# A decode kernel bound by its loads: the result row kept in two PSUM tensors, copied by two engines and stored by SyncE in 16 runs, with the projections summed in place

## Chip, cores, metric

One core of one Trainium2 chip. The metric is device time in microseconds (us) of one execution. "The span" is the time from the first to the last instruction in the profile; the measured time is longer than the span (402.11 against 400.3 us in the profiled run of the kernel before). One TensorE (PE) works with VectorE (DVE), ScalarE (ACT), GpSimd (POOL) and SyncE (SP).

## The reference, cut to what matters

One token of a decoder layer: grouped-query attention over a cache of 65536 keys (32 query heads, 4 key/value heads), and beside it an MLP; both are added to the input row.

```python
def _A_ref(x, k_cache, v_cache, wq, wo):      # attention
    q = (x @ wq)...                           # 32 heads of 128
    p = _softmax(einsum(q, k) * Dh ** -0.5)
    o = einsum(p, v)
    return o.reshape(B, Sq, Hq * Dh) @ wo     # "the projections": one per head
# [... _B_ref: ... gelu(layernorm(x1) @ w3) @ w4 ...]
return x + _A_ref(xn, ...) + _B_ref(xn, ...)  # one row of 1024 bf16
```

## The kernel before

Weights and cache go through three big SBUF slots in a fixed order: wq, w3, w1 and w2, then K and V blocks 0 to 7 (wo before the last V), and at the end w4 in 8 pieces. Everything that is added to the output row is added by matmuls into one PSUM tensor `psB`: the first 512 results on partition 0, the second 512 on partition 32, where PE's two column positions work side by side. Only the projections of the first three groups go elsewhere and are added later.

```python
def row_acc(j, lhsT, rhs, start=False):
    nc.tensor.matmul(psB[32 * j:32 * j + lhsT.shape[1], :], lhsT=lhsT, rhs=rhs, start=start, stop=False,
                     tile_position=(0, 32 * j), skip_group_check=True)
# [...]
def project(g):
    wt = st.tiles["wo"][:].rearrange("p (g j n) -> p g j n", g=HKV, j=8)
    for j in range(8):
        for h2 in range(2):
            if g == HKV - 1:
                row_acc(h2, oT[g][:, j:j + 1], wt[:, g, j, 512 * h2:512 * (h2 + 1)])
                continue
            nc.tensor.matmul(tail["rows"][0:1, h2, :], lhsT=oT[g][:, j:j + 1], rhs=wt[...], ...,
                             tile_position=(0, 0))

def add_projection():
    rows = ppool.tile([1, 2, 512], F32, name="o_rows", tag="p")
    nc.vector.tensor_copy(out=rows[:], in_=tail["rows"][0:1, 0:2, :])
    for j in range(2):
        row_acc(j, ident_f[0:1, 0:1], rows[0:1, j, :])
# [...]
compute_k(NU - 1)
tail["rows"] = ps_S.tile([P, SUBS, 512], F32, name="o_acc", tag="sc")
for g in range(HKV - 1):
    project(g)
add_projection()
compute_v(NU - 1)
early = sum(W4_PIECES[:2])                    # W4_PIECES = (6, 5, 6, 4, 3, 2, 1, 1)
compute_w4(0, early)
project(HKV - 1)
compute_w4(early, FC)

out_t = ogpool.tile([64, 512], BF16, name="out_t", tag="og")
nc.scalar.copy(out=out_t[:], in_=psB[0:64, :])
nc.scalar.dma_start(out=out[0, 0, :].rearrange("(j n) -> j n", j=2),
                    in_=out_t[:].rearrange("(a b) n -> a b n", b=32)[:, 0, :])
```

Of the kernel before, what the change touches and what calls it, by code (L numbers as in the profile page):

```python
# [8 lines left out]
BF16 = mybir.dt.bfloat16  # L9
F32 = mybir.dt.float32  # L10
# [5 lines left out]
P = 128  # L16
ROW = 32768
SUBS = 4
# [45 lines left out]
def kernel(  # L64
# [14 lines left out]
    nc = tc.nc  # L79
# [4 lines left out]
    HKV = A_k_cache.shape[1]  # L84
# [17 lines left out]
    ppool = ctx.enter_context(tc.tile_pool(name="psb", bufs=1))  # L102
    ogpool = ctx.enter_context(tc.tile_pool(name="og", bufs=2))
    ps_S = ctx.enter_context(tc.tile_pool(name="psS", bufs=1, space=bass.MemoryType.PSUM))
# [63 lines left out]
    ident_f = const.tile([P, P], F32, name="ident_f")  # L168
# [9 lines left out]
    for b in range(2):  # L178
        nc.gpsimd.tensor_copy(
            out=spread[:, 2 * b:2 * b + 2, :].rearrange("p r (a i) -> p r a i", a=4),  # L180
            in_=ident_f[:, 64 * b:64 * b + 64].rearrange("p (i r) -> p r i", r=2).unsqueeze(2).to_broadcast([P, 2, 4, 32]))
# [5 lines left out]

    psB = ps_B.tile([P, 512], F32, name="psB")

    def row_acc(j, lhsT, rhs, start=False):  # L190
        nc.tensor.matmul(psB[32 * j:32 * j + lhsT.shape[1], :], lhsT=lhsT, rhs=rhs, start=start, stop=False,  # L191
                         tile_position=(0, 32 * j), skip_group_check=True)

    x_t = ppool.tile([P, DC, 32], BF16, name="x_t", tag="p")
    for a in range(4):
        nc.vector.transpose(out=x_t[32 * a:32 * a + 32].rearrange("p c j -> p (c j)"),  # L196
                            in_=x_row[:, 256 * a:256 * (a + 1)].rearrange("p (i c) -> p c i", c=DC))
# [3 lines left out]
    def layernorm(src, tag):  # L201
# [39 lines left out]
                          in_=sel8[:].unsqueeze(2).to_broadcast([P, 8, 16]))  # L241
# [36 lines left out]
    def place_queries(g):  # L278
        for a in range(4):
            at = slice(32 * a, 32 * a + 32)  # L280
            nc.gpsimd.tensor_copy(  # L281
                out=qdiag[at, LEAD:].rearrange("p (x c) -> p x c", x=4)[:, :, 32 * a:32 * a + 8],
                in_=qx[at, :, 8 * g:8 * g + 8])
# [31 lines left out]
    def compute_k(u):  # L315
        g, b = divmod(u, NB)
        if b == 0:
            place_queries(g)
            group["nball"] = const.tile([P, NB], F32, name=f"nball{g % 2}")
            group["lall"] = const.tile([P, NB], F32, name=f"lall{g % 2}")  # L320
        t = st.tiles[("K", u)]
        cols = t[:].rearrange("p (s u k b x r) -> p s u k b x r", u=SUBS, s=SETS, k=16, b=2, r=2)
        sc = ps_S.tile([P, SUBS, 512], F32, name="sc", tag="sc")
        W = ROW // SETS
        for s in range(SETS):
            words = t[:, W * s:W * (s + 1)].bitcast(F32)
            nc.vector.transpose(out=words, in_=words)  # L327
            for b2 in range(2):
                for r in range(2):
                    c0 = LEAD + P * (2 * b2 + r) - 8 * s  # L330
                    for e in range(SUBS):
                        nc.tensor.matmul(sc[:, e, :], lhsT=qdiag[:, c0:c0 + P], rhs=cols[:, s, e, :, b2, :, r],  # L332
                                         start=(s == 0 and b2 == 0 and r == 0),
                                         stop=(s == SETS - 1 and b2 == 1 and r == 1))
        st.done(("K", u))
        mx = small.tile([P, 1], F32, name="mx")
        nc.vector.reduce_max(out=mx[:], in_=sc[:].rearrange("p e n -> p (e n)"), axis=AX.X)  # L337
        pm = ps_M.tile([P, 512], F32, name="pm_mx", tag="pm")
        nc.tensor.transpose(pm[0:1, 0:P], mx[:, 0:1], ident_f[:])  # L339
        m8 = small.tile([1, 8], F32, name="m8")  # L340
        nc.vector.tensor_reduce(out=m8[:], in_=pm[0:1, 0:P].rearrange("o (j h) -> o h j", h=8), axis=AX.X, op=ALU.max)  # L341
        rep = small.tile([1, P], F32, name="rep")
        nc.vector.tensor_scalar(out=rep[:].rearrange("o (j h) -> o j h", h=8),  # L343
                                in0=m8[:].unsqueeze(1).to_broadcast([1, P // 8, 8]), scalar1=-SCALE, scalar2=None,
                                op0=ALU.mult)
        nc.tensor.transpose(pm[:, P:P + 1], rep[0:1, :], ident_f[0:1, 0:1])  # L346
        nball = group["nball"]
        nc.vector.tensor_copy(out=nball[:, b:b + 1], in_=pm[:, P:P + 1])  # L348
        p_sb = ppool.tile([P, SUBS, 512], BF16, name="p_sb", tag="p")
        nc.scalar.activation(out=p_sb[:], in_=sc[:], func=ACTF.Exp, bias=nball[:, b:b + 1], scale=SCALE,  # L350
                             accum_out=group["lall"][:, b:b + 1])
        flat = p_sb[:].rearrange("p e n -> p (e n)")
        nc.vector.transpose(out=flat, in_=flat)  # L353
        group["p"] = p_sb

    def group_weights():
        nball = group["nball"]
        negmg = small.tile([P, 1], F32, name="negmg")
        nc.vector.tensor_reduce(out=negmg[:], in_=nball[:], axis=AX.X, op=ALU.min)
        wb = small.tile([P, NB], F32, name="wb")  # L360
        nc.scalar.activation(out=wb[:], in_=nball[:], func=ACTF.Exp, bias=negmg[:, 0:1], scale=-1.0)
        og = group["og"]
        nc.vector.tensor_scalar(out=og[:], in0=og[:], scalar1=wb[:, 0:1], scalar2=None, op0=ALU.mult)
        lw = small.tile([P, NB], F32, name="lw")
        ol = small.tile([P, DH + 1], F32, name="ol")
        nc.vector.tensor_tensor_reduce(out=lw[:], in0=group["lall"][:], in1=wb[:], scale=1.0, scalar=0.0,
                                       op0=ALU.mult, op1=ALU.add, accum_out=ol[:, DH:DH + 1])
        return og, wb, ol
# [3 lines left out]
    def compute_v(u):  # L372
        g, b = divmod(u, NB)
        if b == 1:
            og, wb, ol = group_weights()
        vt = st.tiles[("V", u)][:].rearrange("p (s u t d) -> p s u t d", u=SUBS, s=SETS, t=16)
        oacc = ps_O.tile([P, 512], F32, name="oacc")
        pT = group["p"]
        for e in range(SUBS):
            for t in range(16):  # L380
                q = t % 4
                nc.tensor.matmul(oacc[32 * q:32 * (q + 1), :], lhsT=pT[:, e, 32 * t:32 * (t + 1)],  # L382
                                 rhs=vt[:, :, e, t, :], start=(e == 0 and t < 4),
                                 stop=(e == SUBS - 1 and t >= 12), tile_position=(0, 32 * q))
        st.done(("V", u))
        if b == 0:
            og = ogpool.tile([P, 512], F32, name="og", tag="og")
            nc.scalar.copy(out=og[:], in_=oacc[:])
            group["og"] = og
            return  # L390
        nc.vector.scalar_tensor_tensor(out=og[:], in0=oacc[:], scalar=wb[:, 1:2], in1=og[:],  # L391
                                       op0=ALU.mult, op1=ALU.add)
        group_rows(g, og, ol)

    oT = {}
    tail = {}

    def group_rows(g, og, ol):
        pe = ps_M.tile([P, 512], F32, name="pm_e", tag="pm")
# [14 lines left out]
    def project(g):  # L414
        wt = st.tiles["wo"][:].rearrange("p (g j n) -> p g j n", g=HKV, j=8)
        for j in range(8):
            for h2 in range(2):
                if g == HKV - 1:
                    row_acc(h2, oT[g][:, j:j + 1], wt[:, g, j, 512 * h2:512 * (h2 + 1)])
                    continue  # L420
                nc.tensor.matmul(tail["rows"][0:1, h2, :], lhsT=oT[g][:, j:j + 1],  # L421
                                 rhs=wt[:, g, j, 512 * h2:512 * (h2 + 1)], start=(g == 0 and j == 0),
                                 stop=(g == HKV - 2 and j == 7), tile_position=(0, 0))

    def add_projection():
        rows = ppool.tile([1, 2, 512], F32, name="o_rows", tag="p")
        nc.vector.tensor_copy(out=rows[:], in_=tail["rows"][0:1, 0:2, :])  # L427
        for j in range(2):
            row_acc(j, ident_f[0:1, 0:1], rows[0:1, j, :])

    def compute_w4(lo, hi):
        wt = st.tiles["w4"]
# [7 lines left out]
    for u in range(NU - 1):  # L440
        compute_k(u)
        compute_v(u)
    compute_k(NU - 1)
    tail["rows"] = ps_S.tile([P, SUBS, 512], F32, name="o_acc", tag="sc")
    for g in range(HKV - 1):
        project(g)
    add_projection()
    compute_v(NU - 1)
    early = sum(W4_PIECES[:2])
    compute_w4(0, early)  # L450
    project(HKV - 1)
    compute_w4(early, FC)

    out_t = ogpool.tile([64, 512], BF16, name="out_t", tag="og")
    nc.scalar.copy(out=out_t[:], in_=psB[0:64, :])
    nc.scalar.dma_start(out=out[0, 0, :].rearrange("(j n) -> j n", j=2),
                        in_=out_t[:].rearrange("(a b) n -> a b n", b=32)[:, 0, :])

# [1 line left out]
_INS = ['A_x', 'A_k_cache', 'A_v_cache', 'A_wq', 'A_wo', 'B_x', 'B_w1', 'B_w2', 'B_w3', 'B_w4']  # L460
# [26 lines left out]
```

## Time and profile before

Median 402.27 us (402.11 to 402.31, 3 runs). The profiled run took 402.11 us.

| | before |
|---|---|
| span | 400.3 us |
| PE, DVE busy | 59%, 52% |
| loads | 169.87 MB at 424 GB/s, 98.6% of the 16 DMA engines' span |
| last load of w4 lands | 396.73 us |
| last pair of matmuls to issue of the store | 396.77 to 397.80 us |

From the chain that ended last, its end (start us, us, what):

```profile
338.78 40.54 DMA big<-in_A_v_cache_dram
...
379.33 17.39 DMA big<-in_B_w_dram
396.73 0.04 issue
396.77 0.40 PE psB L191 x2
...
397.19 0.58 ACT out_t L455
```

The last V block lands at 379.32, the last piece of w4 at 396.73. From the timeline of the last 34 us, in order (start us, us, engine, line, operation, count, and in brackets idle time before it and what ended it):

```profile
367.50 12.19 PE L421 MATMUL o_acc<-big,oT 128*1 128x512 bf16 x45 [2.40 <-ACT p_sb L350]
...
383.86 1.21 DVE L427 COPY o_rows<-o_acc 1x1024 f32<-1x1024 f32 x1 [13.62 <-PE oacc L382]
385.00 0.73 DVE L391 SCALAR_TENSOR_TENSOR og<-oacc,wb,og 128x512 f32<-128x512 f32 x1
...
386.21 2.30 PE L191 MATMUL psB<-big,hT 128*1 128x512 bf16 x10
...
395.47 1.03 PE L191 MATMUL psB<-big,hT 128*1 128x512 bf16 x6 [0.27 <-DMA big<-in_B_w_dram]
...
396.77 0.38 PE L191 MATMUL psB<-big,hT 128*1 128x512 bf16 x2 [0.27 <-DMA big<-in_B_w_dram]
397.19 0.58 ACT L455 CAST out_t<-psB 64x512 bf16<-64x512 f32 x1 [29.56 <-PE psB L191]
397.80 0.59 ACTq L456 DMA_DIRECT2D out_dram<-out_t  x1
```

The projections (L421) run in PE's wait for V. Then the copy of the projection row (L427) holds up VectorE and, through its adding matmuls, PE (1.33 us of waiting for the copy): the w4 matmuls start only at 386.21. But at 395.47 and 396.77 PE has nothing to do and waits 0.27 us for the DMA each time: it has caught up.

### The profile page before, as it was taken

The page shows a single profiled execution, that of the slowest core. Times are in us where ns is not written, and L with a number is a line of the kernel's source. Part 1 is how long each engine was busy: PE and PEld are TensorE (multiplying, and loading weights), DVE is VectorE, ACT ScalarE, POOL GpSimd, SP SyncE. Part 2 cuts the span into 40 slices and gives each one's busy share as a digit, 9 for nine tenths or more (in the row PEclk, how much of TensorE's full clock was granted, in tenths as well). Part 3 has the DMA queues.
Part 4 walks back from the last instruction along what each step waited for, and adds up shares of the span by engine and source line. Part 5 has one row for each costly group of instructions (what it writes and reads, how often), then busy time and mean ns, then how long its engine had stood idle before and what let it go on. Part 6 is the DMA issues. An engine that isn't in the chain of part 4 may idle for free.

```text
span 400.3 us, 2563 instructions
## 1 busy us (share of the span) xinstructions
PE 236.0 (59%) x1348; PEld 45.2 (11%) x854; DVE 208.9 (52%) x154; ACT 27.3 (7%) x35; POOL 5.3 (1%) x28
## 2 busy tenths in 40 slices
PE   0561960591678247922965195629453946594986
PEld 0210000010200110011102010201020102000222
DVE  1601010965196549644953994279349931975040
ACT  1001010003000200020002000100100020002000
POOL 2000000000000000000000000000000000000000
PEclk9995795597669666978796789568865986697989
DMA  9998999999999999999999999999999998999895
GB/s 419 419 453 371 435 471 458 426 419 419 421 426 465 452 426 414 426 426 432 445 460 426 419 426 419 447 439 452 426 421 426 432 445 385 432 481 426 385 417 201
DMA packets 4575, 170.01 MB, mean 425 GB/s; under 512 B 467, under 2 KB 469, under 8 KB 982
## 3 DMA queue, kind: packets, MB, share of 16 engines
q1 hardware_dynamic: 4560, 169.87, 98.6%
q8 instruction: 8, 0.13, 0.1%
q14 instruction: 1, 0.01, 0.0%
q10 hardware_dynamic: 6, 0.00, 0.0%
HBM read 169.87 MB, written 0.00 MB: 424 GB/s over the span
## 4 chain that ended last, share of the span: by engine, by line
DMA 51%; DVE 26%; PE 16%; ACT 3%; another core or an unknown queue 2%; issue 1%; DVEq 0%; ACTq 0%
DMA big<-in_A_k_cache_dram 31%; DVE big L327 19%; DMA big<-in_A_v_cache_dram 10%; PE sc L332 8%; PE oacc L382 6%; DMA big<-in_A_wq_dram 6%; DMA big<-in_B_w_dram 4%; DVE p_sb L353 3%; DVE mx L337 3%; ACT p_sb L350 3%; PE psq L257 2%; DVE m L341 0%; PE pm_mx L339 0%; PE pm_mx L346 0%
## 5 line engine op out<-in xcount | busy, mean ns | idle before, releaser
L332 PE MATMUL sc<-big,qdiag 128*128 128x512 bf16 x512 | 129.5, 414 | 62.7 <-DVE big L327 57.2
L327 DVE STREAM_TRANSPOSE big<-big 128x4096 f32<-128x4096 f32 x32 | 139.4, 4413 | 49.4 <-DMA big<-in_A_k_cache_dram 49.4
L382 PE MATMUL oacc<-big,p_sb 128*32 128x512 bf16 x512 | 46.9, 539 | 34.5 <-DVE p_sb L353 34.5
L337 DVE TENSOR_REDUCE mx<-sc 128x1 f32<-128x2048 f32 x8 | 18.3, 2291 | 30.0 <-PE sc L332 30.0
L332 PEld LDWEIGHTS <-qdiag 128*128 128x128 bf16 x128 | 13.2, 103 | 174.7 <-issue 145.9
L350 ACT ACTIVATE p_sb<-sc,nball 128x2048 bf16<-128x2048 f32 x8 | 15.7, 1967 | 217.8 <-DVE nball L348 217.8
L353 DVE STREAM_TRANSPOSE p_sb<-p_sb 128x2048 bf16<-128x2048 bf16 x8 | 18.5, 2311 | 18.0 <-ACT p_sb L350 18.0
L382 PEld LDWEIGHTS <-p_sb 128*32 128x32 bf16 x512 | 17.1, 129 | 61.0 <-DVE p_sb L353 35.1
L257 PE MATMUL psh<-big,ln_rep_b 128*32 128x512 bf16 (+1 forms) x64 | 12.4, 941 | 7.6 <-DMA big<-in_B_w_dram 7.6
L421 PE MATMUL o_acc<-big,oT 128*1 128x512 bf16 x48 | 12.8, 437 | 2.4 <-ACT p_sb L350 2.4
L339 PE MATMUL pm_mx<-ident_f,mx 128*1 128x128 f32 x8 | 2.2, 273 | 19.1 <-DVE mx L337 19.1
L296 DVE STREAM_TRANSPOSE h_row<-h_row 128x896 bf16<-128x896 bf16 x1 | 1.1, 1111 | 20.8 <-ACT h_row L295 20.8
L391 DVE SCALAR_TENSOR_TENSOR og<-oacc,wb,og 128x512 f32<-128x512 f32 x4 | 3.0, 746 | 16.7 <-PE oacc L382 16.7
L191 PE MATMUL psB<-big,hT 128*1 128x512 bf16 x56 | 8.1, 424 | 0.6 <-DMA big<-in_B_w_dram 0.5
L427 DVE COPY o_rows<-o_acc 1x1024 f32<-1x1024 f32 x1 | 1.2, 1211 | 13.6 <-PE oacc L382 13.6
L205 PE MATMUL pm_ln<-ln_rowsum_a,ones_f 128*128 128x1 f32 x2 | 0.6, 348 | 12.5 <-DVE ln_rowsum_a L203 12.5
L403 PE MATMUL pm_e<-ol,sel8big 128*128 128x129 f32 x8 | 2.8, 446 | 7.9 <-DVE ol L402 7.9
L257 PE MATMUL psq<-big,ln_rep_a 128*32 128x512 bf16 x64 | 6.2, 573 | 1.5 <-DMA big<-in_A_wq_dram 1.5
L281 POOL COPY qdiag<-qx 32x32 bf16<-32x32 bf16 x16 | 3.2, 203 | 279.5 <-PE sc L332 249.6
L196 DVE STREAM_TRANSPOSE x_t<-x_row 32x256 bf16<-32x256 bf16 x4 | 2.5, 616 | 8.1 <-DMA x_row<-in_A_x_dram 8.0
L269 DVE CAST q_row<-psq 128x512 bf16<-128x512 f32 x1 | 0.7, 691 | 8.4 <-PE psq L257 8.4
L346 PE MATMUL pm_mx<-ident_f,rep 1*128 1x1 f32 x8 | 1.8, 223 | 5.0 <-DVE rep L343 5.0
(95 smaller groups left out, 73.2 us busy)
## 6 DMA issues: line engine op xcount, KB each, us to landing
big<-in_A_wo_dram SPq DMA_DIRECT2D x1, 8192.0 KB, 36.0
big<-in_B_w_dram SPq DMA_DIRECT2D x1, 7168.0 KB, 38.3
big<-in_B_w_dram SPq DMA_DIRECT2D x2, 2048.0 KB, 46.3
big<-in_B_w_dram SPq DMA_DIRECT2D x2, 1536.0 KB, 27.3
big<-in_B_w_dram SPq DMA_DIRECT2D x1, 1280.0 KB, 24.1
big<-in_B_w_dram SPq DMA_DIRECT2D x1, 1024.0 KB
big<-in_B_w_dram SPq DMA_DIRECT2D x1, 768.0 KB, 30.7
big<-in_B_w_dram SPq DMA_DIRECT2D x1, 512.0 KB, 31.5
```

What stands on the lines that cost most here:

```text
L191: nc.tensor.matmul(psB[32 * j:32 * j + lhsT.shape[1], :], lhsT=lhsT, rhs=rhs, start=start, stop=False, tile_position=(0, 32 * j), skip_gro ...
L257: nc.tensor.matmul(acc[32 * q:32 * q + 32, i, 0:n], lhsT=rep[:, c, :], rhs=cols(c, i, q), start=(c == 0), stop=(c == DC - 1), tile_positio ...
L281: nc.gpsimd.tensor_copy(out=qdiag[at, LEAD:].rearrange("p (x c) -> p x c", x=4)[:, :, 32 * a:32 * a + 8], in_=qx[at, :, 8 * g:8 * g + 8])
L327: nc.vector.transpose(out=words, in_=words)
L332: nc.tensor.matmul(sc[:, e, :], lhsT=qdiag[:, c0:c0 + P], rhs=cols[:, s, e, :, b2, :, r], start=(s == 0 and b2 == 0 and r == 0), stop=(s = ...
L337: nc.vector.reduce_max(out=mx[:], in_=sc[:].rearrange("p e n -> p (e n)"), axis=AX.X)
L350: nc.scalar.activation(out=p_sb[:], in_=sc[:], func=ACTF.Exp, bias=nball[:, b:b + 1], scale=SCALE, accum_out=group["lall"][:, b:b + 1])
L353: nc.vector.transpose(out=flat, in_=flat)
L382: nc.tensor.matmul(oacc[32 * q:32 * (q + 1), :], lhsT=pT[:, e, 32 * t:32 * (t + 1)], rhs=vt[:, :, e, t, :], start=(e == 0 and t < 4), stop ...
L391: nc.vector.scalar_tensor_tensor(out=og[:], in0=oacc[:], scalar=wb[:, 1:2], in1=og[:], op0=ALU.mult, op1=ALU.add)
L403: nc.tensor.matmul(pe[:, 0:DH + 1], lhsT=sel8big[:], rhs=ol[:], start=True, stop=True)
L421: nc.tensor.matmul(tail["rows"][0:1, h2, :], lhsT=oT[g][:, j:j + 1], rhs=wt[:, g, j, 512 * h2:512 * (h2 + 1)], start=(g == 0 and j == 0), ...
```

## The change

Its intent: take the copy of the projection row and its adding matmuls away, by summing all projections straight into the running sum; keep the first half of that sum in a PSUM tensor of its own, so that ScalarE and VectorE may copy one half each at the same time; put both halves into one row, and store that row as 16 runs of 128 B, to spread over 16 DMA engines, from SyncE.

```diff
+    tail = {}
+
     def row_acc(j, lhsT, rhs, start=False):
-        nc.tensor.matmul(psB[32 * j:32 * j + lhsT.shape[1], :], lhsT=lhsT, rhs=rhs, start=start, stop=False,
+        at = slice(32 * j, 32 * j + lhsT.shape[1])
+        acc = tail["first"][at, 0, :] if j == 0 and tail else psB[at, :]
+        nc.tensor.matmul(acc, lhsT=lhsT, rhs=rhs, start=start, stop=False,
                          tile_position=(0, 32 * j), skip_group_check=True)
[... project: always row_acc(h2, ...); add_projection is gone ...]
+    first_sum = ogpool.tile([1, 512], F32, name="first_sum", tag="og")
+    nc.vector.tensor_copy(out=first_sum[:], in_=psB[0:1, :])
     compute_k(NU - 1)
-    tail["rows"] = ps_S.tile([P, SUBS, 512], F32, name="o_acc", tag="sc")
+    tail["first"] = ps_S.tile([P, SUBS, 512], F32, name="o_acc", tag="sc")
+    row_acc(0, ident_f[0:1, 0:1], first_sum[:], start=True)
     for g in range(HKV - 1):
         project(g)
-    add_projection()
[...]
-    out_t = ogpool.tile([64, 512], BF16, name="out_t", tag="og")
-    nc.scalar.copy(out=out_t[:], in_=psB[0:64, :])
-    nc.scalar.dma_start(out=out[0, 0, :].rearrange("(j n) -> j n", j=2),
-                        in_=out_t[:].rearrange("(a b) n -> a b n", b=32)[:, 0, :])
+    out_t = ppool.tile([1, 16, 96], BF16, name="out_t", tag="p")
+    nc.scalar.copy(out=out_t[:, 0:8, 0:64], in_=tail["first"][0:1, 0, :].rearrange("o (j n) -> o j n", j=8))
+    nc.vector.tensor_copy(out=out_t[:, 8:16, 0:64], in_=psB[32:33, :].rearrange("o (j n) -> o j n", j=8))
+    nc.sync.dma_start(out=out[0, 0:1, :].rearrange("o (j n) -> o j n", j=16), in_=out_t[:, :, 0:64])
```

More of the change, by code (lines that the diff above doesn't have):

```diff
@@ L395 @@
     oT = {}
-    tail = {}
     def group_rows(g, og, ol):
@@ L417, in project @@
             for h2 in range(2):
-                if g == HKV - 1:
-                    row_acc(h2, oT[g][:, j:j + 1], wt[:, g, j, 512 * h2:512 * (h2 + 1)])
-                    continue
-                nc.tensor.matmul(tail["rows"][0:1, h2, :], lhsT=oT[g][:, j:j + 1],
-                                 rhs=wt[:, g, j, 512 * h2:512 * (h2 + 1)], start=(g == 0 and j == 0),
-                                 stop=(g == HKV - 2 and j == 7), tile_position=(0, 0))
-    def add_projection():
-        rows = ppool.tile([1, 2, 512], F32, name="o_rows", tag="p")
-        nc.vector.tensor_copy(out=rows[:], in_=tail["rows"][0:1, 0:2, :])
-        for j in range(2):
-            row_acc(j, ident_f[0:1, 0:1], rows[0:1, j, :])
+                row_acc(h2, oT[g][:, j:j + 1], wt[:, g, j, 512 * h2:512 * (h2 + 1)])
     def compute_w4(lo, hi):
```

## The prediction

> **What bounds the kernel now.** The stream of weights and cache from HBM. In the 40-slice view the DMA row stands at 9 nearly everywhere, and the queue table gives the SP queue 98.6% of the 16 engines' span: 169.87 MB at 424 GB/s over 400.3 us, against PE 59%, DVE 52%. The chain of waits is 51% DMA and ends: V cache load until 379.32 us, w4 load until 396.73, last pair of w4 matmuls 0.40, ScalarE copy of the result 0.58 (to 397.77); the ScalarE-issued store, at 397.80, ends the span at 400.3. Only a head of about 2 us and the last 3.6 us are not the stream.
>
> **What the change does, by stage.**
>
> 1. Before the last K block VectorE copies half of the running sum (1x512) to SBUF. The 1x1024 copy took 1.21 us, so I estimate 0.65. The instruction order puts it after a transpose ending at 332.15; VectorE then idles 8.35 us until the K block lands: hidden. PE puts the half back with one f32 matmul pair (about 0.6 us, from four that took 1.16) while waiting for V: hidden.
>
> 2. The 48 projections of groups 0 to 2 used one column position; now the halves use two and need 24 more weight loads. The last group's 16 projections, already in that form, took 1.89 us; the 48 took 12.2 us, partly at a reduced clock. I expect 6 to 8 us, done near 375 instead of 380. PE waits there for V in any case.
>
> 3. The 1x1024 copy of the projection row (1.21 us, from 383.86) and its adding matmuls (1.16 us) go. VectorE merges the last group about 1.5 us sooner and PE starts w4 about 2 us sooner. But PE already stood idle for 0.27 us before each of the last two groups of w4 matmuls, waiting for the DMA: it had caught up. The 2 us become longer waits, worth 0 at the end. The loads' order and releases are unchanged (w4 issued at 361.64, when the last K block is freed), so the stream ends at 396.7 as before.
>
> 4. Tail, the only part on the critical path. One 64x512 ScalarE copy (0.58) becomes 1x512 copies by ScalarE and VectorE in parallel. Partitions were parallel already, so nothing shortens: the comparable VectorE 128x512 cast from PSUM took 0.69, so +0.1. The store moves from ScalarE's queue (issue 0.59) to SyncE's (0.33 to 0.52 in this trace): about -0.2. Two 1 KB runs become sixteen of 128 B. [...] For short runs I allow up to +0.2. Net -0.4 to +0.3, centre -0.15.
>
> **Predicted time: 402.1 us**, 401.3 to 402.9 eight times in ten. Faster by over 2%: 1%; within 2%: 98%; slower by over 2%: 1%.
>
> **What would show it.** Last w4 landing at about 396.7; PE waits for w4 longer than 0.27 us each; projections over well before V lands; VectorE's last copy about 0.65 us; span end about 3.5 us after the last landing.
>
> **What would make it wrong.** A store of 128-byte runs that lands much later; a DMA stream that shifts through a release I overlooked; PE slower in the tail through extra weight loads or a lower granted clock.

Two sentences of step 4 are cut: reasons for the number of DMA engines and for the fixed cost of a small transfer that no trace here shows. With them went the inference, used further down, that stores of few runs have the longer issue (0.52 and 0.59 us against 0.33 in this trace). The sum came to -0.4 to +0.3, centre -0.15. The terms that still stand are +0.1 for the copies, about -0.2 for SyncE and up to +0.2 for short runs, together -0.1 to +0.1; for the margin beyond that there is no figure, neither in what is left nor in what is cut. The +0.2 was shown by no trace.

## More of the kernel before

From the page of the profile: the busy row of the DMA engines in 40 slices (tenths, 9 is 90% or more), the queue that carries the loads, and the queue that carries instructions (packets, MB, share of 16 engines).

```profile
span 400.3 us, 2563 instructions
...
DMA  9998999999999999999999999999999998999895
...
q1 hardware_dynamic: 4560, 169.87, 98.6%
q8 instruction: 8, 0.13, 0.1%
```

The loads leave no slice free.

## The result, and the profile after

Median 402.68 us (402.52 to 402.70, 4 runs) against 402.25 us for the kernel before (402.11 to 402.31, 4 runs): a ratio of 1.001, 95% interval 0.9993 to 1.0027, so "same" at the 2% limit. In microseconds it is 0.43 slower, and no run of the one falls into the range of the other. A ratio here is the mean time of one kernel's runs over that of the other's of the same rounds, so it is not quite the ratio of the medians. The interval of these four runs includes 1; the repeat further down, after_again, has 1.0008 to 1.0033.

The same lines of the page as above:

```profile
span 400.7 us, 2585 instructions
...
DMA  9998999999999999999999999999999999999994
...
q1 hardware_dynamic: 4592, 169.87, 98.4%
q8 instruction: 8, 0.13, 0.1%
```

The stream of loads is what it was: in the trace file the last load packet ends at 396.24 us, before at 396.28. The end of the chain that ended last (its last wait for the DMA ends at 395.42; behind that the chain stays on PE):

```profile
363.82 31.55 DMA big<-in_B_w_dram
...
395.42 0.59 PE o_acc L195
...
396.87 0.43 PE o_acc L195
...
397.37 0.68 DVE out_t L450
```

The timeline of the last 36 us, the lines that answer to those of before:

```profile
365.09 8.04 PE L195 MATMUL psB<-big,oT 128*1 128x512 bf16 x24
...
374.00 5.34 PE L195 MATMUL o_acc<-big,oT 128*1 128x512 bf16 x24
...
382.99 0.38 PE L195 MATMUL o_acc<-big,hT 128*1 128x512 bf16 x1
...
383.00 0.75 DVE L395 SCALAR_TENSOR_TENSOR og<-oacc,wb,og 128x512 f32<-128x512 f32 x1 [12.70 <-PE oacc L386]
...
392.26 0.38 PE L195 MATMUL o_acc<-big,hT 128*1 128x512 bf16 x1 [1.02 <-DMA big<-in_B_w_dram]
...
394.16 0.38 PE L195 MATMUL o_acc<-big,hT 128*1 128x512 bf16 x1 [0.87 <-DMA big<-in_B_w_dram]
...
396.71 0.59 PE L195 MATMUL o_acc<-big,hT 128*1 128x512 bf16 x1
...
397.34 0.57 ACT L449 CAST out_t<-o_acc 1x512 bf16<-1x512 f32 x1 [29.64 <-PE psB L195]
397.37 0.68 DVE L450 CAST out_t<-psB 1x512 bf16<-1x512 f32 x1 [10.29 <-PE psB L195]
398.12 0.61 SPq L451 DMA_DIRECT2D out_dram<-out_t  x1
```

Read it from top to bottom. VectorE merges the last group at 383.00 instead of 385.00, and PE starts w4 at 382.99 instead of 386.21. PE then waits for w4 0.73 (not shown), 1.02 and 0.87 us: the lead of 3 us has become waits. The last pair of matmuls starts at 396.71, 0.06 us from where it started before. All of the difference arises behind it: the last matmuls take 0.59 instead of 0.38 us, VectorE's copy 0.68 instead of 0.58, and the store is issued at 398.12 instead of 397.80.

The 0.59 us has a cause in the profile: the granted TensorE clock. Busy time by stretch: stretch, its us, then busy us (and instructions) of PE, weight loads, DVE, ACT and POOL, the granted clock, DMA share and GB/s. First the changed kernel, from 395.00 to the end of the matmuls:

```profile
395.00:397.20 2.20, 2.11 (x10) 0.50 (x7) 0.00 (x0) 0.00 (x0) 0.00 (x0) 0.50 0.26 98
```

and the kernel before, over the same stretch:

```profile
395.00:397.20 2.20, 1.56 (x10) 0.33 (x7) 0.00 (x0) 0.01 (x1) 0.00 (x0) 1.00 0.27 101
```

In the trace files of both kernels the granted clock takes two values, 1.00 and 0.50; in the changed kernel it goes from 1.00 to 0.50 at 394.47 us, behind the waits. So the first theory was:

- **Theory A:** PE, now ahead, waits more, its clock falls, and that costs 0.2 us; the copies and the store cost the other 0.2.
- **Rival B:** the clock does not matter to the time; the copies and the store cost all of the 0.43.

### The profile page after: what moved, and what is told of

It is laid out like the page before. It is cut to its first block, busy times and chain, and to the rows that moved or that the text cites. A ratio compares the mean times of both kernels' runs of the same rounds, so it can differ in the third digit from the quotient of the medians. Undisturbed runs are those within 1.5% of the kernel's fastest.

```text
span 400.7 us, 2585 instructions
## 1 busy us (share of the span) xinstructions
PE 232.7 (58%) x1346; PEld 46.7 (12%) x876; DVE 209.0 (52%) x155; ACT 27.3 (7%) x35; POOL 5.4 (1%) x28
## 4 chain that ended last, share of the span: by engine, by line
DMA 55%; DVE 21%; PE 18%; another core or an unknown queue 2%; ACT 2%; issue 1%; SPq 1%; DVEq 0%; ACTq 0%
DMA big<-in_A_k_cache_dram 42%; DVE big L331 15%; PE sc L336 11%; DMA big<-in_B_w_dram 8%; DMA big<-in_A_wq_dram 5%; PE oacc L386 4%; DVE p_sb L357 2%; DVE mx L341 2%; ACT p_sb L354 2%; PE psq L261 1%; SPq L153 1%; PE o_acc L195 0%; PE pm_mx L343 0%; DVE m L345 0%
## 5 line engine op out<-in xcount | busy, mean ns | idle before, releaser
L386 PE MATMUL oacc<-big,p_sb 128*32 128x512 bf16 x512 | 43.2, 512 | 34.5 <-DVE p_sb L357 34.5
L195 PE MATMUL psB<-big,oT 128*1 128x512 bf16 x32 | 9.9, 479 | 0.0
L195 PE MATMUL o_acc<-big,hT 128*1 128x512 bf16 x28 | 8.2, 425 | 2.8 <-DMA big<-in_B_w_dram 2.6
L195 PE MATMUL o_acc<-big,oT 128*1 128x512 bf16 x32 | 7.2, 379 | 0.0
L195 PEld LDWEIGHTS <-oT 128*1 128x1 bf16 x64 | 5.0, 92 | 10.0 <-issue 4.8
```

The costliest lines, as they stand in the source:

```text
L195: nc.tensor.matmul(acc, lhsT=lhsT, rhs=rhs, start=start, stop=False, tile_position=(0, 32 * j), skip_group_check=True)
L386: nc.tensor.matmul(oacc[32 * q:32 * (q + 1), :], lhsT=pT[:, e, 32 * t:32 * (t + 1)], rhs=vt[:, :, e, t, :], start=(e == 0 and t < 4), stop ...
```

## The experiments

Twelve kernels ran, five rounds each, with the kernel before in the same rounds. "Outside" is the measured time less the span, run by run. The last two columns are read from the profiled run: from the start of the last pair of matmuls to the issue of the store, and from that issue to the measured end (measured time less the issue's start in the trace; it holds an offset that is taken as constant, so only differences count).

| kernel | median us (range) | before, us | span, median | outside, each run | pair to issue | issue to end |
|---|---|---|---|---|---|---|
| before, first profile | 402.25 | | 400.3 | 1.73 to 1.86 (36 runs, all of the sets below) | 1.03 | 4.31 |
| changed, first profile | 402.68 (402.52 to 402.70) | 402.25 | 400.65 | 1.98, 2.28, 1.90, 1.92 | 1.41 | 4.56 |
| inplace_only | 402.33 (402.18 to 403.14) | 402.17 | 400.4 | 1.80, 1.83, 2.84, 1.78, 2.46 | 1.03 | 4.31 |
| tail_only | 402.69 (402.59 to 404.09) | 402.17 | 400.7 | 1.99, 1.99, 1.99, 1.89, 1.97 | 1.20 | 4.56 |
| warm_after | 403.83 (403.71 to 403.94) | 402.17 | 401.9 | 1.91 to 2.04 | 1.19 | 4.57 |
| inplace_warm | 403.52 (402.82 to 403.53) | 402.17 | 401.6 | 1.82 to 1.92 | 1.03 | 4.41 |
| after_again | 402.66 (402.51 to 403.93) | 402.10 | 400.6 | 3.53, 1.91, 1.96, 2.14, 1.97 | 1.19 | late fetch, see there |
| two_runs | 402.48 (402.45 to 402.92) | 402.10 | 400.5 | 1.92 to 1.99 | 1.19 | 4.59 |
| act_store | 402.51 (402.38 to 403.81) | 402.10 | 400.6 | 1.98, 1.84, 1.86, 3.21, 1.91 | 1.20 | 4.61 |
| sync_store | 402.47 (402.37 to 402.55) | 402.10 | 400.3 | 2.10 to 2.17 | 1.03 | 4.68 |
| warm_few | 402.55 (402.38 to 403.67) | 402.15 | 400.6 | 1.95, 1.98, 2.97, 1.93, 1.90 | 1.19 | 4.56 |
| pad_early | 403.47 (403.25 to 403.79) | 402.15 | 401.7 | 1.75 to 1.88 | 1.03 | 4.32 |
| fewer_pe | 402.27 (402.20 to 402.61) | 402.15 | 400.5 | 1.77 to 1.86 | 1.03 | 4.30 |
| trim_after | 402.52 (402.47 to 402.85) | 402.11 | 400.6 | 1.92 to 1.97 | 1.19 | 4.55 |

All kernels passed the comparison with the reference; fewer_pe did so too, within its tolerance, although it leaves out terms.

### inplace_only: the projections alone

The kernel before, with all projections summed in place in `psB`; the old copy and the old store.

```diff
-                if g == HKV - 1:
-                    row_acc(h2, oT[g][:, j:j + 1], wt[:, g, j, 512 * h2:512 * (h2 + 1)])
-                    continue
-                nc.tensor.matmul(tail["rows"][0:1, h2, :], [...])
+                row_acc(h2, oT[g][:, j:j + 1], wt[:, g, j, 512 * h2:512 * (h2 + 1)])
-    add_projection()
```

> The kernel before with one part of the change: all projections summed straight into the running sum, still one PSUM tensor and the old tail (one ScalarE copy of 64x512, a 2-run store from ScalarE). Theory A (PE gets ahead, waits for w4, its granted clock falls to 0.5 at about 394.4 us, so the last matmuls take 0.59 instead of 0.38 us): clock 0.5 in the last 2 us, last pair of matmuls to the copy's start about 0.6 us instead of 0.42, time about 402.45, +0.2 on before. Rival B (only the new copies and the 16-run store cost time): time equal to before, 402.25 within 0.1, and the clock in the tail does not matter.

Measured: 402.33 against 402.17 us, ratio 1.0012 (0.9998 to 1.0025); median span 400.4, that of the kernel before. The end of its timeline:

```profile
365.52 6.62 PE L191 MATMUL psB<-big,oT 128*1 128x512 bf16 x48
...
396.86 0.38 PE L191 MATMUL psB<-big,hT 128*1 128x512 bf16 x2 [0.26 <-DMA big<-in_B_w_dram]
397.28 0.58 ACT L442 CAST out_t<-psB 64x512 bf16<-64x512 f32 x1 [29.16 <-PE psB L191]
397.89 0.59 ACTq L443 DMA_DIRECT2D out_dram<-out_t  x1
```

The clock stayed at 1.00 through the last matmuls here, so this is no test of what a fallen clock costs. It does show that the in-place half of the change gains nothing: the copy and the adding matmuls are gone, and the span is the same. PE's lead was small here, though: it stood idle for 7.41 us before the last V block landed, the clock fell (0.7 on the page for the slice from 380 to 390 us, 1.00 again from 386 us), and the matmuls on V took 6.41 us (3.64 in the changed kernel, at 1.00); w4 started at 385.78, only 0.43 us sooner than before. That a lead of 3 us is worth nothing is shown by the changed kernel, not by this run. Two of five runs were 0.6 to 1 us longer, all of it outside the span; that comes back below.

### tail_only: the copies and the store alone

The kernel before with its row copy and adding matmuls, so with PE as late as before, but with the two PSUM tensors, the two copies and the 16-run store of the changed kernel.

```diff
+    first_sum = ogpool.tile([1, 512], F32, name="first_sum", tag="og")
+    nc.vector.tensor_copy(out=first_sum[:], in_=psB[0:1, :])
     compute_k(NU - 1)
     tail["rows"] = ps_S.tile([P, SUBS, 512], F32, name="o_acc", tag="sc")
+    tail["first"] = tail["rows"][:, 2, :]
+    row_acc(0, ident_f[0:1, 0:1], first_sum[:], start=True)
[... row_acc, copies and store as in the changed kernel ...]
```

> The kernel before with the other part alone: two PSUM tensors, copies by ScalarE and VectorE, 16-run store by SyncE, but the old row copy and adding matmuls kept, so PE stays as late as before. Theory A: granted clock 1.00 until after the last matmul, last pair 0.38 to 0.40 us, and only the copies and the store cost: +0.2, about 402.45. Rival B: the whole +0.43, 402.65 to 402.7.

Measured: 402.69 against 402.17 us, ratio 1.002 (1.0007 to 1.0032), with the clock at 1.00 to the end:

```profile
396.93 0.38 PE L195 MATMUL o_acc<-big,hT 128*1 128x512 bf16 x1 [0.26 <-DMA big<-in_B_w_dram]
...
397.38 0.68 DVE L463 CAST out_t<-psB 1x512 bf16<-1x512 f32 x1 [6.78 <-PE psB L195]
...
398.13 0.60 SPq L464 DMA_DIRECT2D out_dram<-out_t  x1
```

The whole loss is there without any fall of the clock, as rival B had it. From pair to issue it takes 1.20 us where the kernel before takes 1.03; from issue to the measured end 4.56 where before takes 4.31. That is 0.42 us together. One run of 404.09 us had a span of 402.1; the trace at hand is of another run, and what held that one up is open.

### warm_after and inplace_warm: PE kept busy

Idle matmuls in PE's waits for w4, on pieces that have landed, into a PSUM tile that nobody reads: 13 pairs of matmuls, each matmul with its weight load.

```diff
+            for j in range(2):
+                nc.tensor.matmul(tail["idle"][32 * j:32 * j + 1, :], lhsT=hT[:, c:c + 1],
+                                 rhs=wt[:, D * c + 512 * j:D * c + 512 * (j + 1)], start=True, stop=True, [...])
[...]
     project(HKV - 1)
-    compute_w4(early, FC)
+    keep_busy(3, 0)
+    compute_w4(early, 17)
+    keep_busy(4, 12)
+    compute_w4(17, 21)
+    keep_busy(4, 17)
+    compute_w4(21, 24)
+    keep_busy(2, 22)
+    compute_w4(24, FC)
```

> The changed kernel with 13 pairs of idle matmuls (on w4 columns that have landed, into a PSUM tile nobody reads) in PE's waits for w4; the result stays right. Theory A: granted clock 1.00 up to the last matmul, last pair 0.38 to 0.40 us instead of 0.59, time about 402.45, that is 0.2 below the changed kernel. Rival B: the added matmuls change nothing or cost a little: 402.7 or more. Rival C (the clock falls by chance, whatever PE does): clock 0.5 as in the changed kernel.

> In-place projections with the old tail, and the same idle matmuls. Theory A: both costs are gone, time equal to before, 402.25 within 0.1, since the last load's landing bounds it (PE's 2 us lead is worth nothing). Rival B: also 402.25, or somewhat more for the idle matmuls. A gain of over 0.2 us on before would refute the statement that PE's lead is worth nothing at the end.

Measured: 403.83 and 403.52 us, against 402.17. Both expectations failed. The clock was 1.00 to the end, but the last load landed late: the last pair of matmuls started at 398.07 and 398.02, after waits for the DMA. A surprise of over 1 us in a stream whose loads nobody had touched. Among the transfers of warm_after between 393 and 397.5 us is a suspect:

```profile
q8 instruction: 1, 0.02, 1.5%
```

In this stretch the kernel before moves nothing on queue q8. The page gives the two kernels with idle matmuls 9 packets on q8, all other kernels so far 8. In the trace files of the kernel before and of the changed kernel each of the 8 has 16384 bytes and takes 0.91 to 1.10 us. The page calls the queue's kind "instruction", so I take one such packet for the fetch of one block of instructions. The idle matmuls had made the PE program 52 instructions longer (2274 matmuls and weight loads instead of 2222), and the ninth packet moved while the last pieces of w4 were on their way. That the packets bring the PE program was a guess here; fewer_pe below supports it.

- **Theory F1:** that fetch takes one of the 16 DMA engines for about 1 us (1.5% of 16 engines for 4.5 us is 1.08 us of one), and the piece of w4 that waits on that engine lands that much later.
- **Rival F:** the idle matmuls themselves slow the loads.

### pad_early: the same length, nothing added in the tail

The kernel before with 38 idle pairs of weight load and matmul ahead of the first K block in PE's order, far from the tail; 2278 PE instructions by the page's counts.

```diff
     compute_w12()
+    pad = ps_M.tile([P, 512], F32, name="pm_pad", tag="pm")
+    for n in range(38):
+        nc.tensor.matmul(pad[0:1, :], lhsT=hT[:, n % FC:n % FC + 1], rhs=qdiag[:, 0:512], start=True, stop=True, [...])
```

> The kernel before with 38 idle pairs of weight load and matmul at 30 to 60 us from the start, where PE waits for the first K block, so that its PE program is as long as that of the slow idle-matmul try and nothing is added in the tail. Theory F1 (each 16 KB of PE instructions is fetched by one of the 16 DMA engines, about 1.07 us of its time, and a fetch that falls in the last us of the stream delays the last w4 piece): 9 fetches, the ninth at about 395, last pair of matmuls at about 398, time about 403.4, +1.2. Rival F: no change, 402.2.

Measured: 403.47 against 402.15 us, ratio 1.0033 (1.002 to 1.0045). All five runs were over 403.2. The instruction packet between 393.5 and 395.5 us:

```profile
q8 instruction: 1, 0.02, 3.2%
```

3.2% of 16 engines for 2 us is 1.02 us of one engine. What follows, in stretches of its profile (DMA share and GB/s are the last two columns):

```profile
396.50:397.00 0.50, 0.19 (x2) 0.09 (x3) 0.00 (x0) 0.00 (x0) 0.00 (x0) 1.00 0.07 25
397.00:397.90 0.90, 0.78 (x6) 0.17 (x3) 0.00 (x0) 0.00 (x0) 0.00 (x0) 1.00 0.04 16
```

and the same stretches of the kernel before:

```profile
396.50:397.00 0.50, 0.23 (x3) 0.08 (x1) 0.00 (x0) 0.00 (x0) 0.00 (x0) 1.00 0.00 0
397.00:397.90 0.90, 0.15 (x2) 0.00 (x0) 0.00 (x0) 0.58 (x1) 0.00 (x0) 1.00 0.00 0
```

Before, nothing moves after 396.5. Here a share of 0.04 to 0.07, about one engine of sixteen, goes on for another us (in the trace file the load packets from 396.5 on follow one another singly, the last ending at 397.58), and the last pair of matmuls starts at 398.12. At most 0.2 us of that delay came earlier: the last V block landed at 379.50 instead of 379.32. Nothing runs in the tail that did not run before, so rival F falls as the cause of the late landing: the length of the PE program and where its last block falls decide. That the late engine is the one that fetched is inferred from the sizes; the trace does not name engines.

### fewer_pe: one fetch less

Half of the V matmuls of the first four blocks left out, a wrong result: 256 PE instructions fewer, the same loads.

```diff
-        for e in range(SUBS):
+        for e in (range(0, SUBS, SUBS - 1) if u < 4 else range(SUBS)):
```

> The kernel before with half of the V matmuls of the first four blocks left out (a wrong result on purpose), 256 PE instructions fewer, the loads all the same. Theory F1: 7 instruction fetches instead of 8, none after 380 us; the last landing comes earlier by up to 1 us if the eighth fetch, at about 383 us, sat on the DMA engine that finished last, so a time between 401.2 and 402.2. Rival F (fetches do not matter): 402.2, and the last w4 landing as before at 396.7.

Measured: 402.27 against 402.15 us, ratio 1.0004 (0.9992 to 1.0017). The page shows 7 fetches, so 256 PE instructions fewer took one fetch away; but the last pair started at 396.87, no earlier than before. The fetch at about 383 us (383.26 in the kernel before, 1.07 us long) costs nothing at the end. A fetch matters by where it falls.

### after_again, two_runs, act_store, sync_store: the store

All four in the same rounds. after_again is the changed kernel unaltered. The other edits, two_runs and act_store on the changed kernel, sync_store on the kernel before:

```diff
  # two_runs
-    out_t = ppool.tile([1, 16, 96], BF16, name="out_t", tag="p")
+    out_t = ppool.tile([1, 2, 544], BF16, name="out_t", tag="p")
[... copies to out_t[:, 0, 0:512] and out_t[:, 1, 0:512]; the store takes out_t[:, :, 0:512] as 2 runs ...]
  # act_store
-    nc.sync.dma_start(out=out[0, 0:1, :].rearrange([...] j=16), in_=out_t[:, :, 0:64])
+    nc.scalar.dma_start(out=out[0, 0:1, :].rearrange([...] j=16), in_=out_t[:, :, 0:64])
  # sync_store
-    nc.scalar.dma_start(out=out[0, 0, :].rearrange("(j n) -> j n", j=2),
+    nc.sync.dma_start(out=out[0, 0, :].rearrange("(j n) -> j n", j=2),
```

> The changed kernel once more, as the base for the next runs on this chip. Theory A2 (a fixed cost of the tail of 0.24 us from the start of the last pair of matmuls to the end of the span, plus 0.2 us where the granted clock halves before the last matmuls, plus a landing of the last load that scatters by 0.15 us): 0.25 to 0.6 us over before; the span from the last matmul pair's start to its end 3.77 us with the clock at 1.00, 3.99 at 0.5. Rival (all of the 0.43 lies in the clock): about 0.4 over before with the clock at 0.5, equal to before with the clock at 1.00.

> The changed kernel with the row stored as 2 runs of 1 KB by SyncE instead of 16 of 128 B. If short runs cost: issue to end of the span falls from 2.58 to about 2.50 us and the time by 0.05 to 0.1. If the number of runs does not matter: no change, within 0.1 of the changed kernel. If the issue is longer for few runs, as the prediction took it: issue above the 0.61 of the 16-run store.

> The changed kernel with the 16-run store issued by ScalarE instead of SyncE. The prediction held SyncE's issue to be 0.2 us shorter: then this would be 0.2 slower than the changed kernel. By the traces (0.61 on SyncE, 0.59 on ScalarE) it is equal, and the 0.07 us from the copy's end to the issue may fall to 0.03 where ScalarE's own copy ends last, but VectorE's ends last here: 0 to 0.05 faster.

> The kernel before with only its 2-run store moved from ScalarE to SyncE. As the prediction had it: 0.2 faster than before. By the traces: issue 0.6 as before and 0.04 us more from the copy's end to the issue, so equal or 0.05 slower, 402.2 to 402.3.

Measured medians: after_again 402.66, two_runs 402.48, act_store 402.51, sync_store 402.47, the kernel before 402.10 us.

after_again had the same waits of PE for w4 in its trace as the first run, and yet its clock stayed at 1.00 until after the last matmul:

```profile
393.00:397.20 4.20, 2.36 (x16) 0.58 (x13) 0.14 (x1) 0.18 (x1) 0.00 (x0) 1.00 0.54 209
```

So the fallen clock of the first profile is an accident of that run, not a property of the change; two_runs, act_store and trim_after show 1.00 too. Theory A falls as an explanation of the median.

sync_store is the clearest of the four. Its span is that of the kernel before, and its issue is no shorter:

```profile
397.18 0.58 ACT L455 CAST out_t<-psB 64x512 bf16<-64x512 f32 x1 [29.52 <-PE psB L191]
397.79 0.62 SPq L456 DMA_DIRECT2D out_dram<-out_t  x1
```

But it takes 0.37 us more from issue to measured end (4.68 against 4.31), outside the span. Moving the old store to SyncE costs 0.37 where the prediction had a gain of 0.2. The table shows no gain for any version of the store: 4.56 (SyncE, one row, 16 runs), 4.59 (SyncE, one row, 2 runs), 4.61 (ScalarE, one row, 16 runs), 4.68 (SyncE, two partitions), 4.31 (ScalarE, two partitions, before). The two costs do not add. In sum the number of runs hardly matters: 4.56 and 4.59.

Where behind the issue the time goes can be narrowed down. The trace file (trace.npz) also holds the packets of the store and the times at which semaphores change, and these go on behind the last instruction; no view lists the latter. In us from the start of the issue:

| | before | sync_store | trim_after | two_runs |
|---|---|---|---|---|
| issue ends | 0.59 | 0.62 | 0.60 | 0.74 |
| first packet of the store starts | 1.23 | 1.21 | 1.24 | 1.33 |
| last packet ends | 1.32 | 1.30 | 1.40 | 1.42 |
| last signal of its landing | 1.64 | 1.61 | 1.72 | 1.76 |
| last semaphore event in the trace | 4.43 | 4.43 | 4.63 | 4.68 |
| measured end | 4.31 | 4.68 | 4.55 | 4.59 |

(trim_after, described below, is the changed kernel with a shorter program. The measured end holds the constant offset, so it can stand before the last event; compare along a row.) In sync_store the store lands as early as from ScalarE; the whole 0.37 lies outside everything that the trace records, so neither issue nor landing is its cause. In the one-row store of trim_after about 0.09 of the 0.24 us is a later landing, and about 0.12 more arises among the closing semaphore events. What causes either of these last two, 0.37 and 0.12, is open.

For one of the long runs the trace shows a cause. The profiled run of after_again is that of 403.93 us. Its span is 400.4, and between 402.5 and 404 us, two us behind its last instruction, one packet moves, on the instruction queue:

```profile
q8 instruction: 1, 0.02, 5.9%
```

A narrower reading of the same stretch puts its start at about 402.7 us, when the other runs of this kernel are over or nearly so (402.51 to 402.94). In the trace file it lasts from 402.74 to 404.16, and the last semaphore event lies at 402.73, so the fetch is all that the trace shows in the rest of that run. The traces of two_runs and act_store have such a ninth fetch too, but earlier, at 398.1 and 401.3 us, and those runs were of the usual length (402.46 and 402.38). This gave theory F2: the PE program of the changed kernel ends close to the edge of the next block of instructions; in some executions that block is fetched, late, behind the last instruction, and the execution ends later.

### warm_few: PE kept busy without another fetch

The changed kernel with 10 idle matmuls that share three weight loads, 11 PE instructions more by the page's counts (2233 against 2222).

```diff
+            nc.tensor.matmul(tail["idle"][0:1, :], lhsT=hT[:, c:c + 1], rhs=wt[:, D * c:D * c + 512], [...])
[...]
+    compute_w4(early, 17)
+    keep_busy(4, 16)
+    compute_w4(17, 21)
+    keep_busy(4, 20)
+    compute_w4(21, 24)
+    keep_busy(2, 23)
+    compute_w4(24, FC)
```

> The changed kernel with 10 idle matmuls in PE's waits for w4 that share three weight loads (13 instructions more; the earlier try added 52, and its trace shows a ninth instruction fetch of 16 KB inside the last us of the stream). Theory A2 (the clock is worth 0.2, the fetch spoiled the earlier try): granted clock 1.00 to the last matmul, still 8 instruction fetches, last pair 0.38 us, time 0.2 below the changed kernel or 0.25 over before. Rival F (idle matmuls themselves delay the landing, by SBUF or PSUM traffic): the last w4 landing again near 398 and the time near 403.8.

Measured: 402.55 against 402.15 us, ratio 1.0017 (1.0003 to 1.003); 8 fetches, clock 1.00, last pair at 396.80. The late landing of warm_after is gone with the ninth fetch, which again speaks for F1 against F. As a test of the clock it is inconclusive: after_again had 1.00 without any idle matmuls. And the time did not fall below that of the changed kernel by 0.2.

### trim_after: the changed kernel at the old program length

The changed kernel without the 16 matmuls that multiply w2 by a column of zeros (with a single token the shifted rows are all padding, so the result stays right; w2 is still loaded). Its PE program has 2204 matmuls and weight loads, about as many as the kernel before with 2202.

```diff
-        for c in range(DC):
-            for j in range(2):
-                row_acc(j, g_col[:], wt[:, 1, c, 512 * j:512 * (j + 1)])
```

> The changed kernel without the 16 matmuls that multiply w2 by the all-zero column g_col (the result stays right; w2 is still loaded), 18 PE instructions fewer (about 2204, as many as in the kernel before, instead of 2222). Theory F2 (the PE program of the changed kernel ends close to the edge of the next 16 KB of instructions; in the run of 403.93 us a ninth fetch starts 2.3 us after the span's end): no run with more than 2.1 us between the span and the measured time, all five between 402.4 and 402.8, median 402.5. Rival (the outliers have to do with the new copies and the store): one run in four again over 402.9 with 2.1 to 3.5 us outside the span.

Measured: 402.52 (402.47 to 402.85) against 402.11 us, ratio 1.0012 (0.9998 to 1.0025); outside the span 1.92 to 1.97 in all five runs. The end of its timeline:

```profile
396.79 0.38 PE L195 MATMUL o_acc<-big,hT 128*1 128x512 bf16 x1 [0.26 <-DMA big<-in_B_w_dram]
...
397.24 0.68 DVE L447 CAST out_t<-psB 1x512 bf16<-1x512 f32 x1 [10.07 <-PE psB L195]
397.98 0.60 SPq L448 DMA_DIRECT2D out_dram<-out_t  x1
```

This is as theory F2 expected, but at the 7 in 29 below, five clean runs come by chance one time in four, and this set ran on another chip than the long programs; F2 is supported, not shown. Over all runs the pattern is: programs of 2218 to 2233 PE instructions had more than 2.1 us outside the span in 7 of 29 runs (after, inplace_only, after_again, two_runs, act_store, warm_few); those of 2206 and fewer in none of 51 (36 of the kernel before, and tail_only, fewer_pe, trim_after; sync_store, where all five lie at 2.10 to 2.17, is left out); those of 2270 and more, whose ninth fetch falls inside the span, in none of 15. A late ninth fetch in a long run was seen in one trace, that of 403.93 us; for the other long runs it is inferred.

With the accidents taken out, trim_after shows what the change itself costs: +0.41 us, 0.16 of it from the last pair to the issue (1.19 against 1.03) and 0.24 behind the issue (4.55 against 4.31).

No version beat the kernel before.

## Why the prediction was right or wrong

The range and the class were right; the sign of the small difference was wrong (-0.15 predicted, +0.43 measured), and the net range that the sum of step 4 gave, -0.4 to +0.3, was missed. The stated range of 1.6 us held it.

- **"The stream ends at 396.7 as before": right.** The last pair of matmuls starts at 396.77 before, 396.71 after, and between 396.57 and 396.93 in all kernels without a ninth fetch in the stream. The in-place projections are worth nothing at the end, alone (inplace_only).
- **Step 1, the copy of half the sum, 0.65 us and hidden: right.** It took 0.64 us at 330.75, with VectorE idle for 9.04 us afterwards. The matmul pair took 1.0 us rather than 0.6, hidden as well.
- **Step 2, projections in 6 to 8 us, done near 375: wrong, without effect on the time.** They ran from 365.09 to 379.34. PE ran all 24 of the second half first (8.04 us, at a granted clock of 0.50 until 370.57) and all 24 of the first half, whose PSUM buffer ScalarE's exponential had still to read (365.45 to 367.42), after them (5.34 us, at 1.00); so the two column positions never worked side by side. In inplace_only, where they alternate, 48 took 6.62 us.
- **Step 3, w4 started sooner and worth 0: right.** 3.2 us sooner; the waits grew to 0.73, 1.02 and 0.87 us.
- **Step 4, "About -0.2" for moving the store to SyncE: the step that failed.** It was read from the durations of issues, 0.33 to 0.52 us on SyncE against 0.59 on ScalarE; but those of SyncE belonged to loads of other shapes. SyncE's issue of this store took 0.61 us, and that of the old store 0.62: the engine makes no gain. In sync_store the issue is 0.03 us longer and the landing no later, yet the end comes 0.37 us later, outside the trace. Instead of -0.2, the time from issue to end grew by 0.24 to 0.25 with the store in its new form: about 0.09 of it the landing, the rest not explained. The inference that few-run stores have the longer issue holds from one row (0.74 with 2 runs, 0.60 to 0.61 with 16), but 2 runs from two partitions took 0.62 (sync_store).
- **Step 4, the copies, +0.1: right in kind, short by 0.06.** VectorE's copy took 0.68 against ScalarE's 0.58; the start came 0.03 later behind the last pair, and the wait between copy and issue grew from 0.03 to 0.06 or 0.07. Together 0.16. VectorE's 0.68 is what the prediction's comparison, a 128x512 cast in 0.69 us, had given; the 0.06 is the later start and the longer wait.
- **Step 4, 16 engines for 16 runs, at most +0.2 for short runs: the 16 packets are shown, neither the 16 engines nor the cost.** Behind 397 us the changed kernel moves 32 packets (in the trace file 16 of 128 B and 16 of 4 B, with 16 separate landing signals); the kernel before moved 4 (2 of 1024 B, 2 of 4 B):

Changed kernel, packets from 397 us on:

```profile
DMA packets 32, 0.00 MB, mean 1 GB/s; under 512 B 32, under 2 KB 32, under 8 KB 32
```

Kernel before, the same:

```profile
DMA packets 4, 0.00 MB, mean 1 GB/s; under 512 B 2, under 2 KB 4, under 8 KB 4
```

  In the trace files up to seven of the 32 packets are under way at one time, and up to three of the 4; which engines carry them the trace does not say, so 16 engines were not shown. For 2 KB from one row the 16 runs gain and cost next to nothing: 4.56 and 4.59 us with 16 and 2 runs.
- **"A lower granted clock", named as a risk: seen once, and not the cause.** It added about 0.2 us from pair to issue in the first profile (1.41 against 1.19), and 1.00 was granted in after_again.

## What to carry to other kernels

Here the loads bound the kernel (98.6% of the DMA engines' span): work that was taken off PE became waits (w4 started 3.2 us sooner, and the waits grew to 0.73, 1.02 and 0.87 us), and only the steps behind the last landing were left to shorten. Cost those from the step that ends last, and take the length of an issue from a transfer of the same shape (0.33 to 0.52 us for loads on SyncE, 0.61 for this store). Splitting a copy over two engines gained nothing here, since partitions were already parallel (0.58 us for 64 partitions, 0.57 and 0.68 for one): the slower engine then set the time. And when an edit that should be harmless moves the end by a us, look at the instruction fetches: in pad_early a longer PE program put one at about 394 us, near the end of a saturated stream, and it was not hidden (+1.32 us).
